# A new order of a kernel's pieces: score groups together, zeros up to the first transposes, later blocks of k loaded from SyncE's queue

## The chip, the core and the metric

The kernel runs on one core of a Trainium2 chip. The metric is device time in microseconds (us); the program launches once per run. The core has a matrix engine (TensorE, PE in the profile, with PEld for its weight loads), a vector engine (VectorE, DVE), an activation engine (ScalarE, ACT), a general engine (GpSimd, POOL) and SyncE (SP), which here only issues DMAs. Each works through its own list of instructions in order, and they wait for each other by semaphores. Matmul results go to PSUM, eight banks of 512 floats in each of 128 partitions.

## The reference

Two layers follow each other: a recurrent attention with decay, and a channel mix.

```python
for t in range(S):                       # q, k, v: 4 batches, 8 heads, 768 tokens, 64 wide
    state = gamma * state + outer(k[t], v[t])
    y[t] = 0.125 * q[t] @ state
x = y, heads side by side                # 4 x 768 x 512
x_prev = x shifted by one token
xk = mu_k * x + (1 - mu_k) * x_prev      # xr the same with mu_r
k = relu(xk @ w_k)                       # 512 -> 1024
out = sigmoid(xr @ w_r) * ((k * k) @ w_v)
```

## The kernel before

The 4 x 768 tokens are cut into 12 blocks n of 256 tokens, three to a batch. The recurrence is done in chunks of 128 tokens (u = 0 and 1 of a block): scores within a chunk, masked, and a state carried from chunk to chunk.

All work is cut into pieces, and the constant `ORDER` (lines 16 to 68) is the list of them, written out by hand: a loop at its end (lines 518 to 530) calls one function for each word. Every engine executes its pieces in the order of the words, and nothing reorders them. A word is a code, its numbers, and after @ the PSUM banks that it writes; T.4.1@0 is the transposition of k of block 4 into bank 0. The codes are:

- lk, lq, lv (lines 178 to 185): load k, q, v of a block. k stays in 32 bits; q and v are cast to 16 bits on the way. lk.n alone is issued by SP, lk.n.2 by POOL, lq and lv always by POOL. There are four buffers of each. wk, wr, wv, mu: weights and mixing factors (wk and wv in two halves), from POOL; mu from ACT.
- ks: k scaled by powers of the decay, on VectorE for blocks 0 to 2, on POOL from 3 on. gy: a table of powers, on VectorE.
- T.n.1 and Tq.n: PE transposes k (128x128) and q (64x64); E.n.1 and E.n.0 copy these to SBUF on ACT.
- S.n.i: scores of block n (i: even or odd tokens as keys), I.n: the part of y from the carried state; C.n: the new state; Y.n: the rest of y. All are runs of 64x64 matmuls on PE.
- M.n.i: VectorE masks the scores. U.n.u and G.n.u: state summed (VectorE) and decayed (POOL). D.n: y scaled into x. dx.n: x minus its neighbour (POOL, VectorE for blocks 0 and 1). X.n.w.j0.j1: VectorE mixes xk (w = 0) or xr (w = 1), columns j0 to j1.
- K.n.g: keys, eight matmuls of 128x256; Q.n.g: relu and square on ACT. R.n.t: gate; s.n.t: its sigmoid on ACT. V.n.t.p: values, first or second half of the sum. O.n.t: product on VectorE; st.n.t: store, from SP.
- Block 0 has the halves apart (Du, du, Xu, Ku, Qu), block 11 its last product (Vc, Oc, sc). S.0 and T.0 are in two halves.
- z.c: c matmuls of zeros whose result nobody reads (lines 481 to 486). mt, me: mu transposed by PE and copied by ACT.

In SBUF, ks, qT, kT, the masked scores, xk and xr have three buffers each, dx two, the gates and outputs five. A piece that writes a PSUM bank waits until what was in it has been read. DMAs from POOL use eight semaphores in turn, so each waits until the one eight before it has landed.

Of the kernel before, what the change touches and what calls it, by code (L numbers as in the profile page):

```python
# [13 lines left out]

KSC = 64.0
ORDER = """
lk.0.0.0.2 lk.0.0.2.4 lq.0 mu lv.0 gy wk.0 lk.1.2 ks.0.0.0.2 z.7@0 mt@0 lq.1 me ks.0.0.2.4
T.0.1.0.2@1 lv.1 E.0.1.0.2 T.0.1.2.4@0 E.0.1.2.4 wk.1 z.2@2 Tq.0@23 wr E.0.0 wv.0 z.4@4
S.0.0.0.2@23 C.0@01 wv.1 M.0.0.0.2 S.0.0.2.4@45 M.0.0.2.4 U.0.0 z.5@6 I.0.0@45 U.0.1 S.0.1.0.2@23
S.0.1.2.4@67 lk.2.2 M.0.1.0.2 M.0.1.2.4 G.0.1 z.5@0 Y.0 ks.1.0 lq.2 Du.0.0 z.4@1 T.1.1@6 lv.2  # L20
Tq.1@23 du.0.0.0 E.1.1 Xu.0.1.0.0.1 z.2@0 C.1@01 lk.3.2 Xu.0.1.0.3.4 E.1.0 Xu.0.1.0.2.3
Xu.0.1.0.1.2 Xu.0.0.0.3.4 Xu.0.0.0.0.1 z.2@7 S.1.0@23 Xu.0.0.0.1.2 M.1.0 lq.3 Xu.0.0.0.2.3 U.1.0
z.7@4 Ku.0.0.0@4 Du.0.1 G.1.0 du.0.0.1 I.1.0@23 Qu.0.0.0 S.1.1@67 Ku.0.1.0@0 Xu.0.1.1.0.1
Xu.0.1.1.2.3 lv.3 Xu.0.1.1.1.2 R.0.0@4 Xu.0.1.1.3.4 Qu.0.1.0 Xu.0.0.1.3.4 Xu.0.0.1.0.1
Xu.0.0.1.1.2 R.0.1@0 Xu.0.0.1.2.3 s.0.0 M.1.1 Ku.0.1.1@5 s.0.1 lk.4.2 U.1.1 Y.1 Qu.0.1.1 G.1.1
Ku.0.0.1@1 D.1 V.0.0.0@0 Qu.0.0.1 lq.4 dx.1.0 V.0.0.1 V.0.1.0@1 X.1.1.3.4 lv.4 X.1.1.1.2 X.1.1.2.3
V.0.1.1 X.1.1.0.1 ks.2.0 R.1.0@2 lq.5 Tq.2@45 X.1.0.0.1 s.1.0 T.2.1@3 X.1.0.1.2 lk.5.2 E.2.0 C.2@2
X.1.0.2.3 R.1.1@6 U.2.0 E.2.1 X.1.0.3.4 O.0.0 G.2.0 K.1.3@7 s.1.1 O.0.1 ks.3.1 st.0.0 I.2.0@23
Q.1.3 S.2.1@45 st.0.1 S.2.0@01 M.2.1 K.1.0@6 lv.5 T.3.1@7 M.2.0 Q.1.0 C.3@45 lq.6 K.1.1@6 E.3.1
U.3.0 lk.6.2 U.3.1 Y.2 Q.1.1 ks.4.1 Tq.3@67 D.2 K.1.2@5 E.3.0 V.1.0.0@4 Q.1.2 dx.2.1 S.3.0@67  # L30
I.3.0@23 S.3.1@01 M.3.0 T.4.1@5 V.1.0.1 G.3.1 E.4.1 M.3.1 lk.8.2 V.1.1.0@6 X.2.1.2.3 lv.6 V.1.1.1
X.2.1.3.4 X.2.1.1.2 lk.7.2 C.4@01 X.2.1.0.1 Y.3 X.2.0.1.2 lq.7 R.2.0@5 X.2.0.2.3 X.2.0.3.4
X.2.0.0.1 lv.7 R.2.1@7 s.2.0 U.4.0 O.1.1 G.4.0 K.2.1@5 s.2.1 O.1.0 ks.5.1 st.1.1 Tq.4@67 D.3 Q.2.1
st.1.0 K.2.2@0 E.4.0 U.4.1 K.2.0@5 dx.3.1 Q.2.2 I.4.0@67 S.4.1@01 S.4.0@23 Q.2.0 M.4.1 T.5.1@4
ks.6.1 K.2.3@5 E.5.1 M.4.0 V.2.0.0@0 Q.2.3 G.4.1 V.2.1.0@1 lk.9.2 X.3.1.0.1 X.3.1.1.2 V.2.0.1
X.3.1.3.4 lq.8 X.3.1.2.3 V.2.1.1 X.3.0.0.1 lk.10.2 X.3.0.3.4 Y.4 X.3.0.2.3 X.3.0.1.2 C.5@5 Tq.5@23
U.5.0 ks.8.1 K.3.3@4 E.5.0 O.2.1 O.2.0 K.3.0@5 st.2.1 Q.3.3 D.4 st.2.0 G.5.0 K.3.1@4 Q.3.0 ks.7.1
I.5.0@01 S.5.0@67 S.5.1@23 Q.3.1 M.5.0 T.6.1@5 K.3.2@4 E.6.1 dx.4.1 M.5.1 V.3.0.0@6 Q.3.2 R.3.1@7
lk.11.2 X.4.1.1.2 V.3.1.0@4 X.4.1.0.1 s.3.1 X.4.1.2.3 lv.8 R.3.0@7 X.4.1.3.4 X.4.0.0.1 lq.9
X.4.0.2.3 R.4.1@5 s.3.0 X.4.0.1.2 X.4.0.3.4 V.3.1.1 s.4.1 K.4.1@5 O.3.1 K.4.3@7 st.3.1 Q.4.1  # L40
C.6@45 Tq.6@23 Q.4.3 U.6.0 ks.9.1 Y.5 U.6.1 V.3.0.1 E.6.0 D.5 K.4.2@7 G.6.1 O.3.0 dx.5.1 S.6.0@01
Q.4.2 st.3.0 I.6.0@23 S.6.1@45 M.6.0 R.4.0@6 T.7.1@7 M.6.1 s.4.0 lv.9 K.4.0@0 E.7.1 lq.10
X.5.1.2.3 T.8.1@1 X.5.1.3.4 Q.4.0 Y.6 X.5.1.1.2 C.7@67 X.5.1.0.1 lv.10 Tq.7@45 E.8.1 X.5.0.1.2
V.4.0.0@0 X.5.0.0.1 lq.11 E.7.0 X.5.0.2.3 V.4.0.1 X.5.0.3.4 U.7.0 ks.10.1 D.6 K.5.2@1 K.5.3@6
Q.5.2 O.4.0 G.7.0 K.5.1@1 st.4.0 Q.5.3 dx.6.1 U.7.1 V.4.1.0@0 Q.5.1 K.5.0@6 G.7.1 R.5.1@1 Q.5.0
X.6.1.0.1 X.6.1.1.2 S.7.0@67 X.6.1.2.3 I.7.0@23 s.5.1 S.7.1@45 X.6.1.3.4 V.4.1.1 M.7.0 R.6.0@1
X.6.0.2.3 V.5.1.0@6 X.6.0.0.1 s.6.0 X.6.0.3.4 V.5.1.1 X.6.0.1.2 O.4.1 V.5.0.0@7 O.5.1 st.4.1 M.7.1
V.5.0.1 st.5.1 R.5.0@6 Y.7 s.5.0 Tq.8@45 O.5.0 lv.11 C.8@6 K.6.1@0 E.8.0 U.8.0 st.5.0 D.7 G.8.0
K.6.3@1 Q.6.1 ks.11.1 I.8.0@45 S.8.1@23 Q.6.3 S.8.0@67 M.8.1 K.6.0@0 dx.7.1 K.6.2@1 M.8.0 Q.6.0
# [12 lines left out]
Q.10.3 Y.11 K.10.2@3 D.11 R.9.1@0 Q.10.2 dx.11.1 R.10.1@3 s.9.1 K.10.1@4 s.10.1 X.11.1.0.1
V.9.0.0@3 Q.10.1 X.11.1.3.4 X.11.1.1.2 K.9.2@4 X.11.1.2.3 X.11.0.2.3 V.10.0.0@5 X.11.0.1.2 Q.9.2
X.11.0.0.1 V.10.1.0@4 X.11.0.3.4 K.11.3@0 V.10.0.1 Q.11.3 V.10.1.1 O.10.0 K.11.1@0 st.10.0 O.10.1
R.11.0@1 st.10.1 Q.11.1 K.11.0@0 s.11.0 V.9.0.1 Q.11.0 V.9.1.1 O.9.0 K.11.2@0 st.9.0 O.9.1
R.11.1@1 st.9.1 Q.11.2 V.11.0.0@0 s.11.1 V.11.0.1 Vc.11.1.0@1 O.11.0 Vc.11.1.1@2 st.11.0 Oc.11.1.0
sc.11.1.0.0 Oc.11.1.1 sc.11.1.1.1
"""


# [1 line left out]
def kernel(  # L72
# [13 lines left out]
    B, H, S, D = q.shape  # L86
# [3 lines left out]
    C = 128  # L90
    TM = 2 * C
    NJ = H // 2
# [57 lines left out]
    ident = c16[:, 0:P]  # L150
# [45 lines left out]
    def turned(n, a, j0=0):  # L196
        return banks("T", n, a, j0).bitcast(F16)
# [14 lines left out]
                            Q16(n)[:, 2 * j + hp, i * D : i * D + D], ident,  # L212
                        )

    def trans_q(n):
        pt = turned(n, 0)[:, :, 0 : 2 * NJ * D].rearrange("p u (j i t) -> p u j i t", j=NJ, i=2)
        for j in range(NJ):
            for i in range(2):
                for u in range(2):
                    r = slice(u * D, u * D + D)  # L220
                    for hp in range(2):
                        nc.tensor.transpose(  # L222
                            pt[hp * D : hp * D + D, u, j, i, :],
                            Q16(n)[r, 2 * j + hp, i * D : i * D + D], ident[r, r],
                        )

    def transed(n, a, j0=0, j1=NJ):
        pt = turned(n, a, j0)
        if len(BANK["T", n, a, j0]) == 2:
            pt = pt[:, :, 0 : 2 * NJ * D].rearrange("c u (j i p) -> c u j p i", j=NJ, i=2)  # L230
            out = QT(n).rearrange("c j u (p i) -> c u j p i", i=2)
        elif a == 0:
            pt = pt.rearrange("c (j i p) -> c j p i", j=NJ, i=2)[:, j0:j1]
            out = QT(n)[:, j0:j1].rearrange("c j u (p i) -> c j (u p) i", i=2)
        else:
            pt = pt.rearrange("c (j i p) -> c j i p", j=NJ, i=2)[:, j0:j1]
            out = KT(n)[:, j0:j1]
        nc.scalar.copy(out=out, in_=pt)  # L238
# [265 lines left out]
    def load_wv(h):  # L504
# [5 lines left out]
        "S": scores, "M": masked, "C": state, "U": summed, "G": decayed, "I": inter, "Y": intra,  # L510
        "D": yout, "dx": differ, "X": mixed, "K": keys, "Q": squared, "R": gate, "s": opened,
        "V": values, "O": result, "st": store, "gy": powers, "wk": load_wk, "wr": load_wr,
        "wv": load_wv, "mu": load_mu, "mt": trans_mu, "me": copy_mu, "z": zeros, "Tq": trans_q,
        "Du": yout_u, "du": differ_u, "Xu": mixed_u, "Ku": keys_u, "Qu": squared_u,
        "Vc": values_c, "Oc": result_c, "sc": store_c,
    }
# [1 line left out]
    for word in ORDER.split():  # L518
        word, _, at = word.partition("@")
        code, *args = word.split(".")  # L520
        args = tuple(int(x) for x in args)
        if at:
            key = args
            if code in ("T", "Tq"):
                code_key, key = "T", (args[0], args[1] if code == "T" else 0, (args[2:] + (0,))[0])
            else:
                code_key = code
                key = {"I": args[:1], "S": args[:2] + (args[2:] + (0,))[:1]}.get(code, args)
            BANK[(code_key,) + key] = [int(x) for x in at]
        CODES[code](*args)  # L530
# [30 lines left out]
```

## Time and profile before

| | us |
|---|---|
| median of 3 runs | 162.99 (162.97, 162.99, 164.17) |
| the profiled execution | 164.16 |
| its span | 162.4 |
| PE busy in it | 153.6 |
| VectorE busy | 116.5 |
| ACT busy | 94.3 |
| POOL busy | 80.5 |

The profile is of one execution. A start time counts from the beginning of the span. In a group's line stand its start, the time from the first start to the last end, engine, line, operation, tiles and count; in square brackets is how long the engine had been idle and what released it. Matmuls overlap, so a group's length is more than its distance to the next group. In the lines by slices each digit is the busy share of one fortieth of the span in tenths.

### The profile page before, as it was taken

What the parts mean: (1) busy time and instruction counts of PE and PEld (TensorE: products, weight loads), DVE (VectorE), ACT (ScalarE), POOL (GpSimd) and SP (SyncE); (2) the same over time, 40 slices, a digit from 0 to 9 for tenths busy, and PEclk for the clock granted to TensorE, in tenths of its full rate; (3) what the DMA queues carried; (4) which work ended last, traced back from release to release, by engine and by line L of the source; (5) the groups of instructions that cost most, each with busy time, mean ns of one, the idle gap of its engine ahead of it and who ended that gap; (6) DMA issues with size and microseconds to landing.
All of it is one profiled execution on the core that took longest, in us unless ns stands there. A gap on an engine that the chain in (4) does not pass through costs nothing.

```text
span 162.4 us, 5592 instructions
## 1 busy us (share of the span) xinstructions
PE 153.6 (95%) x2479; PEld 99.4 (61%) x2479; DVE 116.5 (72%) x209; ACT 94.3 (58%) x148; POOL 80.5 (50%) x79
## 2 busy tenths in 40 slices
PE   7499999999999999999969999999999999999992
PEld 2245577458657668566836558458568668666661
DVE  2518997988598688948997957927998979364222
ACT  3230438378727929767829418686467937774740
POOL 7938435629999969909786009303216140130000
PEclk9999999999999999999999999999999999999999
DMA  5999999999999989294694036211030011000333
GB/s 149 168 254 197 205 211 249 247 246 253 269 230 229 239 167 299 39 215 129 81 172 96 4 129 111 23 69 65 6 124 10 4 69 40 25 4 0 129 129 129
DMA packets 34167, 21.98 MB, mean 135 GB/s; under 512 B 25816, under 2 KB 29792, under 8 KB 34144
## 3 DMA queue, kind: packets, MB, share of 16 engines
q0 software_dynamic: 29184, 14.68, 60.7%
q1 hardware_dynamic: 4512, 6.69, 11.5%
q8 instruction: 19, 0.31, 0.8%
q10 hardware_dynamic: 448, 0.26, 0.6%
q14 instruction: 4, 0.03, 0.1%
HBM read 24.25 MB, written 6.29 MB: 188 GB/s over the span
## 4 chain that ended last, share of the span: by engine, by line
PE 81%; DVE 7%; ACT 5%; DMA 2%; issue 1%; ACTq 1%; POOL 0%; DVEq 0%
PE ps L395 23%; PE ps L421 22%; PE ps L409 12%; PE ps L246 5%; PE ps L483 4%; PE ps L315 3%; PE ps L204 3%; PE ps L302 3%; DMA mu<-in_moe_mu_r_dram 2%; DVE xk L358 2%; PE ps L222 2%; ACT qT L238 2%; PE ps L271 2%; ACT kr L402 1%; PE ps L375 1%
## 5 line engine op out<-in xcount | busy, mean ns | idle before, releaser
L395 PE MATMUL ps<-xk,wk 128*128 128x256 f16 x352 | 44.1, 273 | 1.7 <-DVE xk L358 1.6
L421 PE MATMUL ps<-wv,k 128*128 128x512 f16 x184 | 43.7, 379 | 0.0
L395 PEld LDWEIGHTS <-wk 128*128 128x128 f16 x352 | 33.4, 98 | 10.2 <-issue 2.1
L253 DVE TENSOR_TENSOR a<-ps,c_sb 128x1024 f16<-128x1024 f32 (+1 forms) x26 | 28.8, 1138 | 13.3 <-PE ps L246 6.5
L402 ACT ACTIVATE kr<-ps 128x512 f32<-128x512 f32 x44 | 26.1, 593 | 18.0 <-PE ps L395 18.0
L344 POOL TENSOR_TENSOR dx<-xT 128x1024 f32<-128x1024 f32 x10 | 18.9, 1892 | 20.3 <-DVE xT L329 20.3
L405 ACT ACTIVATE k<-kr 128x512 f16<-128x512 f32 x44 | 27.7, 630 | 1.4
L421 PEld LDWEIGHTS <-k 128*128 128x128 f16 x184 | 17.3, 98 | 18.3 <-ACT k L405 0.4
L427 DVE SCALAR_TENSOR_TENSOR os<-ps,rs 128x512 f32<-128x512 f32 x23 | 15.4, 686 | 14.5 <-PE ps L421 5.9
L415 ACT ACTIVATE rs<-ps 128x512 f32<-128x512 f32 x24 | 14.2, 593 | 18.4 <-PE ps L409 15.2
L409 PE MATMUL ps<-wr,xr 128*128 128x512 f16 x96 | 23.9, 380 | 0.0
L358 DVE SCALAR_TENSOR_TENSOR xr<-dx,mu,xT 128x256 f16<-128x256 f32 (+1 forms) x52 | 21.0, 465 | 4.0 <-POOL dx L344 3.9
L358 DVE SCALAR_TENSOR_TENSOR xk<-dx,mu,xT 128x256 f16<-128x256 f32 (+1 forms) x52 | 23.4, 510 | 0.0
L189 POOL TENSOR_TENSOR ks<-k,csm_sb 128x1024 f16<-128x1024 f32 x9 | 17.1, 1905 | 5.1 <-PE ps L271 5.1
L290 POOL TENSOR_TENSOR tg<-t,csm_sb 128x256 f16<-128x256 f32 x16 | 10.0, 622 | 18.2 <-DVE t L287 18.1
L238 ACT COPY kT<-ps 128x1024 f16<-128x1024 f16 (+1 forms) x13 | 12.1, 940 | 8.7 <-PE ps L204 8.7
L176 POOL DMA_DIRECT2D v<-in_v_dram x12 | 10.9, 906 | 11.5 <-PE ps L222 9.1
L329 DVE TENSOR_TENSOR xT<-ps,gy_sb 128x1024 f32<-128x1024 f32 x11 | 13.4, 1219 | 4.1 <-ACT kr L402 2.9
L238 ACT COPY qT<-ps 128x1024 f16<-128x1024 f16 x12 | 12.1, 1007 | 6.1 <-PE ps L222 6.1
L409 PEld LDWEIGHTS <-xr 128*128 128x128 f16 x96 | 8.8, 98 | 9.1 <-DVE xr L358 0.3
L483 PE MATMUL ps<-zero 128*128 128x512 f16 x38 | 13.0, 480 | 1.2 <-DVE xT L467 1.2
L176 POOL DMA_DIRECT2D q<-in_q_dram x12 | 11.0, 913 | 2.5 <-DMA wk<-in_moe_w_k_dram 1.6
(43 smaller groups left out, 142.4 us busy)
## 6 DMA issues: line engine op xcount, KB each, us to landing
out_dram<-os SPq DMA_DIRECT2D x23, 256.0 KB, 2.1
k<-in_k_dram POOLq DMA_DIRECT2D x11, 512.0 KB, 8.6
q<-in_q_dram POOLq DMA_DIRECT2D x12, 256.0 KB, 8.1
v<-in_v_dram POOLq DMA_DIRECT2D x12, 256.0 KB, 7.3
wk<-in_moe_w_k_dram POOLq DMA_DIRECT2D x2, 512.0 KB, 10.8
wv<-in_moe_w_v_dram POOLq DMA_DIRECT2D x2, 512.0 KB, 16.6
k<-in_k_dram SPq DMA_DIRECT2D x2, 256.0 KB, 3.5
wr<-in_moe_w_r_dram POOLq DMA_DIRECT2D x1, 512.0 KB, 14.4
```

The costliest lines, as they stand in the source:

```text
L176: eng.dma_start(out=d(n)[:, 2 * j0 : 2 * j1], in_=rows(x, n)[:, 2 * j0 : 2 * j1])
L189: (nc.vector, nc.gpsimd)[e].tensor_tensor(out=KS(n)[:, :, h0:h1], in0=K32(n)[:, h0:h1].rearrange("p h (i d) -> p i h d", i=2), in1=gks[:, ...
L238: nc.scalar.copy(out=out, in_=pt)
L253: nc.vector.tensor_tensor(out=A2(n)[:, i, :, j0:j1], in0=pairs(banks("S", n, i, j0))[:, :, j0:j1], in1=causal[:, i, None, None, :].to_broa ...
L344: (nc.vector, nc.gpsimd)[e].tensor_tensor(out=DX(n)[:, j0:j1, t0:t1], in0=x[:, j0:j1, c + t0 : c + t1], in1=x[:, j0:j1, c - 1 + t0 : c - 1 ...
L358: nc.vector.scalar_tensor_tensor(out=XM[w](n)[:, j, t0:t1], in0=DX(n)[:, j, t0:t1], scalar=mu[:, w * NCO + j : w * NCO + j + 1], in1=x[:, ...
L395: nc.tensor.matmul(pz[:, i, :], lhsT=wk16[:, co, fo * P : fo * P + P], rhs=XM[0](n)[:, co, :], start=(i == 0 and co == 0), stop=(co == NCO ...
L402: nc.scalar.activation(out=kr, in_=banks("K", n, g).rearrange("p (i t) -> p i t", i=2), func=AF.Relu)
L405: nc.scalar.activation(out=K2(n)[:, 2 * g : 2 * g + 2], in_=kr, func=AF.Square)
L409: nc.tensor.matmul(banks("R", n, tb), lhsT=XM[1](n)[:, co, tb * P : tb * P + P], rhs=wr16[:, co, :], start=(co == 0), stop=(co == NCO - 1),)
L421: nc.tensor.matmul(banks("V", n, tb, 0), lhsT=K2(n)[:, fo, tb * P : tb * P + P], rhs=wv16[:, fo, :], start=(fo == 0), stop=(fo == NFO - 1),)
L483: nc.tensor.matmul(banks("z", count), lhsT=zero[:, 0:P], rhs=zero, start=True, stop=True, skip_group_check=True,)
```

## The change

The list `ORDER` is written anew; with the six pieces named below apart, every piece other than the zeros occurs in both lists with the same numbers, while banks and places differ. At the start:

```diff
-lk.0.0.0.2 lk.0.0.2.4 lq.0 mu lv.0 gy wk.0 lk.1.2 ks.0.0.0.2 z.7@0 mt@0 lq.1 me ks.0.0.2.4
-T.0.1.0.2@1 lv.1 E.0.1.0.2 T.0.1.2.4@0 E.0.1.2.4 wk.1 z.2@2 Tq.0@23 wr E.0.0 wv.0 z.4@4
-S.0.0.0.2@23 C.0@01 wv.1 M.0.0.0.2 S.0.0.2.4@45 M.0.0.2.4 U.0.0 z.5@6 I.0.0@45 U.0.1 S.0.1.0.2@23
-S.0.1.2.4@67 lk.2.2 M.0.1.0.2 M.0.1.2.4 G.0.1 z.5@0 Y.0 ks.1.0 lq.2 Du.0.0 z.4@1 T.1.1@6 lv.2
+lk.0.0.2.4 lk.0.0.0.2 lq.0 lv.0 lv.1 lk.1.2 ks.0.0.2.4 lq.1 ks.0.0.0.2 wk.1 gy z.10@1 T.0.1.0.2@0
+T.0.1.2.4@1 E.0.1.0.2 wk.0 mu wr z.4@4 Tq.0@23 E.0.1.2.4 lk.2.2 E.0.0 wv.0 z.5@4 S.0.0.0.2@23
+S.0.0.2.4@01 C.0@45 M.0.0.0.2 U.0.0 lq.2 M.0.0.2.4 z.2@6 I.0.0@23 S.0.1.0.2@67 U.0.1 S.0.1.2.4@01
+M.0.1.0.2 G.0.1 M.0.1.2.4 ks.1.0 z.5@4 Y.0 Du.0.0 z.1@4 C.1@01 mt@6 U.1.0 T.1.1@2 Du.0.1 G.1.0 me
```

The two halves of S.0.0 follow each other, and C.0 comes after both. S.1.0, I.1.0 and S.1.1 follow each other, where a group of keys stood between the first two. Y, C and Tq of a block and its neighbours stand together in most blocks. mt and its load move behind the first transposes. On PE the order around blocks 0 to 4 becomes:

```diff
-z.7@4 Ku.0.0.0@4 I.1.0@23 S.1.1@67 Ku.0.1.0@0 R.0.0@4 R.0.1@0 Ku.0.1.1@5 Y.1 Ku.0.0.1@1 V.0.0.0@0
-V.0.0.1 V.0.1.0@1 V.0.1.1 R.1.0@2 Tq.2@45 T.2.1@3 C.2@2 R.1.1@6 K.1.3@7 I.2.0@23 S.2.1@45 S.2.0@01
-K.1.0@6 T.3.1@7 C.3@45 K.1.1@6 Y.2 Tq.3@67 K.1.2@5 V.1.0.0@4 S.3.0@67 I.3.0@23 S.3.1@01 T.4.1@5
+I.1.0@45 S.1.1@67 Ku.0.1.1@0 Ku.0.0.1@2 z.1@3 Ku.0.0.0@0 R.0.0@2 Y.1 T.2.1@3 Ku.0.1.0@0 V.0.1.0@0
+V.0.0.0@1 R.0.1@4 Tq.2@67 C.2@3 K.1.2@2 K.1.3@4 K.1.1@5 S.2.0@23 I.2.0@67 K.1.0@4 V.0.0.1 S.2.1@23
+T.3.1@4 V.0.1.1 Y.2 C.3@23 Tq.3@45 R.1.0@0 V.1.0.0@1 S.3.0@23 I.3.0@45 S.3.1@67 R.1.1@0 V.1.0.1
```

Later in the list, attention runs further ahead of the channel mix: 22 groups of keys, gates and values follow Y.11 in the list before, 32 in the new one. The loads of k of blocks 6 to 11 lose their .2, so SP issues them, among the stores:

```diff
-st.0.0 st.0.1 st.1.1 st.1.0 st.2.1 st.2.0 st.3.1 st.3.0 st.4.0 st.4.1
+lk.6 st.0.0 st.0.1 st.1.0 lk.7 st.1.1 lk.10 lk.8 lk.9 st.2.0 st.2.1 st.3.0 st.4.0 st.3.1 lk.11 st.4.1
```

POOL's list around blocks 2 to 4 becomes:

```diff
-lq.4 lv.4 lq.5 lk.5.2 G.2.0 ks.3.1 lv.5 lq.6 lk.6.2 ks.4.1 dx.2.1 G.3.1 lk.8.2 lv.6 lk.7.2 lq.7 lv.7 G.4.0 ks.5.1
+lv.4 lq.4 lq.6 G.2.0 ks.3.1 lk.5.2 lv.5 ks.6.1 G.3.1 ks.4.1 dx.2.1 lq.5 lv.7 lv.6 G.4.0 ks.5.1
```

The functions change only so that a code Tk, which transposes k in 64x64 pieces, would be understood. No word of the new list uses it.

```diff
-    def trans_q(n):
-        pt = turned(n, 0)[:, :, 0 : 2 * NJ * D].rearrange("p u (j i t) -> p u j i t", j=NJ, i=2)
+    def trans_small(n, a):
+        pt = turned(n, a)[:, :, 0 : 2 * NJ * D].rearrange("p u (j i t) -> p u j i t", j=NJ, i=2)
...
+    def trans_q(n):
+        trans_small(n, 0)
+
+    def trans_k(n):
+        trans_small(n, 1)
```

## The prediction

> **What bounds the kernel now.** I read the page's shares first, then the chain of waits, then TensorE's timeline and, beside it, what each DMA's issue says of its landing.
>
> ```profile
> span 162.4 us, 5592 instructions
> ...
> PE 153.6 (95%) x2479; PEld 99.4 (61%) x2479; DVE 116.5 (72%) x209; ACT 94.3 (58%) x148; POOL 80.5 (50%) x79
> ...
> PE   7499999999999999999969999999999999999992
> ...
> DVE  2518997988598688948997957927998979364222
> ...
> DMA  5999999999999989294694036211030011000333
> ...
> PE 81%; DVE 7%; ACT 5%; DMA 2%; issue 1%; ACTq 1%; POOL 0%; DVEq 0%
> ```
>
> TensorE holds the chain. From 22 us on it hardly idles: eight key matmuls take 0.87 us per group, four value or gate matmuls 0.86, wherever they stand. Such work can't shrink by reordering; only holes, filler and switches can. The filler stands in the first 22 us (timeline of PE):
>
> ```profile
> 1.19 3.17 PE L483 MATMUL ps<-zero 128*128 128x512 f16 x7 [1.19 <-DVE xT L467]
> 6.46 0.24 PE L476 MATMUL ps<-csm_sb,mu 8*128 8x8 f32 x1 [2.10 <-DMA mu<-in_moe_mu_r_dram]
> 6.63 1.03 PE L204 MATMUL ps<-c_sb,ks 128*128 128x128 f16 x8
> 7.46 1.06 PE L483 MATMUL ps<-zero 128*128 128x512 f16 x2
> 8.45 0.64 PE L222 MATMUL ps<-c_sb,q 64*64 64x64 f16 x32
> 9.02 1.89 PE L483 MATMUL ps<-zero 128*128 128x512 f16 x4
> 10.84 0.43 PE L246 MATMUL ps<-qT,kT 64*64 64x128 f16 x8
> 11.84 1.69 PE L483 MATMUL ps<-zero 128*128 128x512 f16 x5
> 14.02 1.25 PE L483 MATMUL ps<-zero 128*128 128x512 f16 x5
> ```
>
> Seven zeros end, TensorE idles 2.10 us for mu, and the zeros stay slow: successive starts are 427 ns apart until 12.67 us and 217 ns after 12.94. The first scores (I call their start s, 10.84 here) come 0.69 us after their last input, the copy of qT that ends at 10.15; four slow zeros stand in between.
>
> One stall is no property of the order:
>
> ```profile
> 80.03 4.33 DVE L358 SCALAR_TENSOR_TENSOR xk<-dx,mu,xT 128x256 f16<-128x256 f32 x4
> 84.41 2.45 PE L395 MATMUL ps<-xk,wk 128*128 128x256 f16 x21 [1.62 <-DVE xk L358]
> ```
>
> One of these four took 3.15 us instead of 0.48, and TensorE's group 2.65 instead of 0.87: 1.78 us. The profiled execution was 164.16 (span 162.4 plus 1.76 around it); without that stall 162.4, against the median 162.99. I count changes from 162.99, since two of the three times are 162.97 and 162.99; from 162.4 all would be 0.6 lower.
>
> **The change, part by part.**
>
> Start up to s. `mt` and its wait leave the front; ten zeros of 0.427 us run from 1.19 to 5.46. The scaling of k now precedes `gy`: the loads land at 3.96 and 5.07 (issue 0.74 and 1.21, 3.2 and 3.9 to landing), so the two 0.69 us scalings end near 4.7 and 5.8, and T starts at 5.86 instead of 6.63. On ACT mu's two issues (0.58 + 0.27) now stand between the two copies of kT: the second ends near 8.3 to 8.6. Tq waits for q, which lands at 7.52 (1.25 + 6.26). Copying qT takes 1.0, so s can't be before 9.3 to 9.55. Whether it gets there depends on the zeros between Tq and the scores, five now: 2.1 us slow, 1.1 fast.
>
> [...] The row: 6.2 us of work from 6.46 came before the fast pitch. If that repeats from 5.86, z.4 and z.5 are slow, Tq ends at 9.0 and s is 11.1, 0.3 later than now. [...] I take release by 8 us at 3 in 4: s moves by -1.3 (ends -1.5 and +0.3).
>
> From s to block 4. Worked on each queue from the rows (M half 0.60, ks 1.13, half D 0.70, Xu 0.264, X 0.397, full D or M 1.14, E 0.9, Q 1.17, ks on POOL 1.87): U.0.0 ahead of the second M ends at s+1.6 rather than s+2.2; ks.1.0 ends at s+5.1, not s+5.6; D.1 starts at s+15.65 with ks.2.0 done already, where now it starts at s+16.85 without. VectorE is thus nearly 2 us ahead. TensorE is not: it waits 0.6 us for xk before Ku.0.1.1, 0.5 for bank 2, 0.4 for xk before Ku.0.0.0, and 0.85 at V.0.1.0@0, which follows Ku.0.1.0@0 in the same bank and has the 0.6 us relu with two handovers in front of it. T.4.1 starts at s+33.9 with V.1.0.1 done; now at s+33.2 without it (0.86). Net gain 0.16.
>
> POOL's early pieces, in the order of landing. Saturated, its queue spaces landings by 1.55 us for a k, 1.24 for a q, 1.5 for a v and 2.55 for a weight. v1 now goes ahead of k1, and wk's halves behind q1, so k1 lands near 12.7 (needed for ks.1.0 at s+3.9, 13.4), q1 13.9 (Tq.1, 15.8), wk.1 16.5 (Ku.0.1.1, 19.7), wk.0 19.1 (21.1), wr 21.7 (R.0.0, 23.3), k2 23.2 (ks.2.0, 23.7), wv.0 25.8 (V.0.1.0, 27.3). Least cover is 0.5 us, at k2; a late k2 would hold VectorE's U.1.1 and D.1, and through dx.1.0 the keys of block 1. An issue also waits for the landing of the issue eight before it: G.0.1 now stands behind q2, which waits for v1 (about 11.1) and is issued by 12, before U.0.1 is done (s+2.6). G.1.0 stands in front of v2, k3 and wv.1 and waits for U.1.0 (s+6.1, 15.7); those transfers would start moving only after wv.0 anyway, so it costs nothing. ks.6.1 ahead of G.3.1 and ks.4.1 waits for C.3 on TensorE and for lk.6; behind it are G.3.1, ks.4.1 and dx.2.1, and for ks.4.1 waits T.4.1: counted among the rivals.
>
> VectorE's late pieces. X.11.0 comes right behind D.11 and waits some 2 us for POOL's dx.11.1 (1.89), with three pieces of X.10.0 behind it. K.10.0 needs these 5.3 us after Y.11; seven groups (6.0 us) stand before it. Nothing lost, 0.7 of cover.
>
> Switches. A group ahead of a run of 64x64 matmuls takes 0.96 instead of 0.86, so a switch costs 0.1 us. The runs go from 33 to 30: 0.3 us, most of it inside the 0.16 above. Zeros go from 38 to 37, which by itself is nothing, as they fill waits.
>
> Block 4 to the end. Now the small holes are 0.41 at I.4.0 with 0.1 to 0.2 beside it. In the new order I find C.6@23 0.17 (Q.3.2 ahead of Q.3.3 on ACT), V.4.0.0 0.27, I.7.0@23 0.2, V.5.1.0@6 0.3, K.7.2 0.15, R.9.0@1 0.16, V.10.0.0 0.15: 1.4, against 0.6, less what the first blocks save at I.4.0. At S.8.0 the new order stands, work for work, 0.25 ahead of the old relative to s, and loses about 0.3 by the end: zero. The tail is the same work behind Vc; its wait for Q.11.3 is covered by R.11.0 and V.11.0.0 (1.73 against 1.3).
>
> k from SP. Six issues of 0.91 leave POOL: 5.4 us, all where POOL has slack (it waits 20.3 us for xT and 18.1 for t in all), so worth nothing directly. [...] Cover 0.2 and 0.9; ends 0 and +1; I take 0. Behind lk.6 on SP stand only stores, the first due at 38 us; lk.8 to lk.10 hold store 2.0 no longer than ks.5.1 (s+42, store due at s+49).
>
> Sum: -1.3 + 0.0 = -1.3: 161.7.
>
> **The rivals.**
>
> Clock released late. For it: the row above. Against: the 2.1 us idle is gone. s = 10.8 to 11.1: 162.9 to 163.3, no change.
>
> Just-in-time handovers lost, on the slower side. The new order leaves many arrivals with under 0.1 us: ks.4.1 behind ks.6.1 and G.3.1 on POOL (4.3 us of work in the 4.7 between C.3 and T.4.1), K.2.1 on xk, S.6.0 on U.6.1, R.4.1 on U.7.0, K.7.0 on its relu, about a dozen. Each late one stalls TensorE and all behind it, since nothing is reordered. From 0.11 us each the gain is gone; between 0.16 and 0.41, the two like waits of now (Tq.3 on ACT's kr at 41.0 us; I.4.0), it costs 1.9 to 4.9: 163.6 to 166.6, and as not all slip I put 164.9. For it: DVE shares of 8 and 9 until 125 us. Against: the present order is as tight and lost 1 us.
>
> [...]
>
> The change does less than it says: the small-transposition of k is coded but no word of the order uses it, and three switches fewer is 0.3 us. If also the zeros change nothing, 163.
>
> More gain: s = 9.3 from the 162.4 base, or a stall like that at 81 us seldom: 160.8.
>
> **How the numbers follow.** Clock early and handovers held 0.50 (161.7, own range 160.9 to 162.5); clock late or little changed 0.20 (163.0); handovers or loads lost 0.20 (164.9); more gain 0.10 (160.8). A measurement of this kernel tells about 1% (1.6 us) from no change. Faster by over 1% is under 161.36: a third of the first case, most of the last, and a little for the uncertain base: 0.30. Slower is over 164.62: most of the third and a rest: 0.19. Range 160.5 to 164.7.
>
> **What the changed profile would show.** Zeros at a 217 ns pitch before 9 us, T at 5.9, first scores at 9.3 to 9.6; Ku.0.1.0 and V.0.1.0 with a hole of 0.8 between; T.4.1 near 43.5; a store or k of SP landing in 6 us or more before 45 us; POOL with some 75 us busy. Wrong if scores start after 10.8, if holes of over 0.2 us on PE sum to more than 2 us after 45 us, or if TensorE waits for wv or v.

## The result, and the profile after

The changed kernel takes 161.34 us (median; 160.77 to 161.76) against 162.98 for the kernel before on the same chip: 0.9884 of it, 95% interval 0.9843 to 0.9925. A second series gave 161.33 against 163.09, 0.9894 (0.9859 to 0.993). So it gains 1.6 to 1.8 us, close to the 1% that counts as told apart from no change. The forecast was 161.7.

The profiled execution of after took 161.76, that of before 164.16. The latter lay 1.2 us above its own median, so distances between these two traces are too large by about that much, and I read places rather than totals from them. Both traces of the changed kernel are the slowest executions of their series (161.76 of four, 162.03 of six), so waits read from them are those of a late execution. From the page of after:

```profile
span 159.5 us, 5601 instructions
...
PE 151.9 (95%) x2478; PEld 98.8 (62%) x2478; DVE 116.7 (73%) x209; ACT 93.6 (59%) x148; POOL 75.1 (47%) x73
...
DMA  5999999999999999475159991100030000510153
...
PE 65%; DMA 18%; DVE 7%; POOL 5%; issue 2%; POOLq 0%; DVEq 0%
```

The last line is the one to stop at. DMA's share of the chain has gone from 2% to 18%. GpSimd is busy 75.1 us, as forecast. The chain in order of time (start, length, what) names two transfers:

```profile
6.53 12.81 DMA wk<-in_moe_w_k_dram
...
22.17 16.05 DMA q<-in_q_dram
...
38.27 0.44 PE ps L221 x32
```

The second is q of block 3: GpSimd issued it at 22.17, it landed at 38.22, and Tq.3 starts on it 0.05 later. Here is TensorE's timeline, the start first and then the places where it stood still before block 4, with the group in which a wait was forecast:

```profile
1.19 4.45 PE L494 MATMUL ps<-zero 128*128 128x512 f16 x10 [1.19 <-DVE xT L478]
5.89 1.03 PE L203 MATMUL ps<-c_sb,ks 128*128 128x128 f16 x8 [0.25 <-DVE ks L188]
6.71 1.10 PE L494 MATMUL ps<-zero 128*128 128x512 f16 x4
7.97 0.45 PE L221 MATMUL ps<-c_sb,q 64*64 64x64 f16 x32 [0.16 <-DMA q<-in_q_dram]
8.35 1.25 PE L494 MATMUL ps<-zero 128*128 128x512 f16 x5
9.54 0.42 PE L257 MATMUL ps<-qT,kT 64*64 64x128 f16 x16
...
24.68 0.62 PE L203 MATMUL ps<-c_sb,ks 128*128 128x128 f16 x8 [0.29 <-DVE ks L188]
25.13 1.06 PE L386 MATMUL ps<-xk,wk 128*128 128x128 f16 x16
26.03 1.89 PE L432 MATMUL ps<-wv,k 128*128 128x512 f16 x8
...
38.27 0.44 PE L221 MATMUL ps<-c_sb,q 64*64 64x64 f16 x32 [0.67 <-DMA q<-in_q_dram]
```

The start went as forecast: transposes at 5.89, zeros at the fast pitch of 217 ns from 7.0 us on, first scores (s) at 9.54 against 10.84. (The page's clock row reads 9 in every slice, before and after, so it is the pitch that shows the change.) But two holes follow that the forecast's sum did not have: 0.29 at T.2.1, for which it had only named k of block 2 as its least cover, and 0.67 at Tq.3. And one that it had is not there: V.0.1.0 at 26.03 follows Ku.0.1.0 at 25.13 without a wait. That is a misreading of mine. The list has Ku.0.1.0@1; the prediction, and the diff shown ahead of it, have @0.

Events by trace, in us (landings are the issue's start plus the trace's time to landing):

| | s | k of block 2 landed | T.2.1 | q of block 3 landed | Tq.3 | T.4.1 | end of PE |
|---|---|---|---|---|---|---|---|
| before | 10.84 | 28.34 | 33.29 | 33.79 | 41.03 | 44.03 | 159.17 |
| after | 9.54 | 23.37 | 24.68 | 38.22 | 38.27 | 43.00 | 156.15 |
| after, second series | 10.04 | 24.41 | 25.72 | 38.53 | 38.57 | 43.30 | 156.47 |

T.4.1 in after stands with V.1.0.1 (0.86 us of TensorE) already done, in before without it.

### The profile page after: what moved, and what is told of

Its sections match the earlier page's. It is cut to its first block, busy times and chain, and to the rows that moved or that the text cites. A ratio compares the mean times of both kernels' runs of the same rounds, so it can differ in the third digit from the quotient of the medians.

```text
span 159.5 us, 5601 instructions
## 1 busy us (share of the span) xinstructions
PE 151.9 (95%) x2478; PEld 98.8 (62%) x2478; DVE 116.7 (73%) x209; ACT 93.6 (59%) x148; POOL 75.1 (47%) x73
## 4 chain that ended last, share of the span: by engine, by line
PE 65%; DMA 18%; DVE 7%; POOL 5%; issue 2%; POOLq 0%; DVEq 0%
PE ps L432 21%; PE ps L406 19%; PE ps L420 11%; DMA q<-in_q_dram 10%; DMA wk<-in_moe_w_k_dram 8%; DVE xr L369 4%; PE ps L257 3%; PE ps L326 3%; PE ps L203 2%; PE ps L313 2%; POOL v L175 2%; PE ps L221 2%; PE ps L282 1%; DVE xk L369 1%; POOL q L175 1%
## 5 line engine op out<-in xcount | busy, mean ns | idle before, releaser
L432 PE MATMUL ps<-wv,k 128*128 128x512 f16 x184 | 45.2, 379 | 0.1
L406 PE MATMUL ps<-xk,wk 128*128 128x256 f16 x352 | 42.6, 273 | 0.1
L406 PEld LDWEIGHTS <-wk 128*128 128x128 f16 x352 | 33.9, 98 | 7.3
L369 DVE SCALAR_TENSOR_TENSOR xr<-dx,mu,xT 128x256 f16<-128x256 f32 (+1 forms) x52 | 25.3, 518 | 2.1 <-POOL dx L355 2.1
L420 PE MATMUL ps<-wr,xr 128*128 128x512 f16 x96 | 24.8, 379 | 0.5 <-DVE xr L369 0.5
L369 DVE SCALAR_TENSOR_TENSOR xk<-dx,mu,xT 128x256 f16<-128x256 f32 (+1 forms) x52 | 22.9, 478 | 3.0 <-POOL dx L355 3.0
L494 PE MATMUL ps<-zero 128*128 128x512 f16 x37 | 11.5, 451 | 1.2 <-DVE xT L478 1.2
## 6 DMA issues: line engine op xcount, KB each, us to landing
k<-in_k_dram SPq DMA_DIRECT2D x6, 512.0 KB, 11.3
```

The source lines that it names most:

```text
L369: nc.vector.scalar_tensor_tensor(out=XM[w](n)[:, j, t0:t1], in0=DX(n)[:, j, t0:t1], scalar=mu[:, w * NCO + j : w * NCO + j + 1], in1=x[:, ...
L406: nc.tensor.matmul(pz[:, i, :], lhsT=wk16[:, co, fo * P : fo * P + P], rhs=XM[0](n)[:, co, :], start=(i == 0 and co == 0), stop=(co == NCO ...
L420: nc.tensor.matmul(banks("R", n, tb), lhsT=XM[1](n)[:, co, tb * P : tb * P + P], rhs=wr16[:, co, :], start=(co == 0), stop=(co == NCO - 1),)
L432: nc.tensor.matmul(banks("V", n, tb, 0), lhsT=K2(n)[:, fo, tb * P : tb * P + P], rhs=wv16[:, fo, :], start=(fo == 0), stop=(fo == NFO - 1),)
```

## The experiments

My theory on going in was that of the forecast: the earlier s is the gain, all that follows moves with it, and k issued from SyncE is worth nothing. The rivals: the front is held by deliveries, whatever s is; and k from SyncE is itself the gain.

**The start alone, in the old order.**

```diff
-lk.0.0.0.2 lk.0.0.2.4 lq.0 mu lv.0 gy wk.0 lk.1.2 ks.0.0.0.2 z.7@0 mt@0 lq.1 me ks.0.0.2.4
+lk.0.0.2.4 lk.0.0.0.2 lq.0 lv.0 wk.0 lk.1.2 ks.0.0.2.4 ks.0.0.0.2 gy z.10@4 lq.1
...
+mt@7 me T.1.1@6
```

> The order of before with nothing but the changed start: k loaded and scaled ahead of gy, ten zeros straight up to the transposes, mu and its transposition behind them. Theory (the start sets when the first scores begin, and all that follows comes earlier by as much): first scores at 9.5 to 9.8 us instead of 10.84, time 161.6 to 161.8 against 163.0 for before (ratio near 0.992). Rival (the gain comes from the order behind the start): scores early, but the time stays at 162.6 to 163.2, since weights or k arrive no earlier and the wait only moves.

162.41 (162.06 to 163.17), 0.9964 of before (0.9935 to 0.9993): 0.6 to 0.8 gained, not 1.3. s came at 8.78, T.4.1 at 41.30, 2.7 earlier than in before's trace, so in the old order the front does follow the start: q of block 3 landed at 33.80 there, long before Tq.3 asked for it at 38.3. Then a part was lost in the middle of one group of keys, and the profile names nothing that the engine waited for (TensorE's timeline of this kernel):

```profile
49.13 1.04 PE L394 MATMUL ps<-xk,wk 128*128 128x256 f16 x8
51.45 0.50 PE L394 MATMUL ps<-xk,wk 128*128 128x256 f16 x3 [1.28 <-issue]
```

What made that wait is open, and so is whether other executions have it; this one, 162.38, is at the median.

**The old start in the changed order**: seven zeros, the wait for mu in front again, and two and four zeros behind the transposes.

```diff
-lk.0.0.2.4 lk.0.0.0.2 lq.0 lv.0 lv.1 lk.1.2 ks.0.0.2.4 lq.1 ks.0.0.0.2 wk.1 gy z.10@1 T.0.1.0.2@0
+lk.0.0.0.2 lk.0.0.2.4 lq.0 mu lv.0 gy lv.1 lk.1.2 ks.0.0.0.2 z.7@6 mt@6 me lq.1 ks.0.0.2.4 wk.1
```

> The changed order with the start of before: mu and gy first, seven zeros, the wait for mu in front of the transposes. Theory (start worth 1.3, the rest worth 0.3 to 0.6): first scores at 10.6 to 11.0, time 162.4 to 162.7 (ratio 0.996 to 0.998). Rival (the rest carries the gain): 161.3 to 161.6.

161.46 (161.09 to 161.71), 0.9905 (0.9876 to 0.9935): the changed kernel's time. TensorE:

```profile
10.69 0.42 PE L257 MATMUL ps<-qT,kT 64*64 64x128 f16 x16
...
25.48 0.62 PE L203 MATMUL ps<-c_sb,ks 128*128 128x128 f16 x8
...
38.15 0.49 PE L221 MATMUL ps<-c_sb,q 64*64 64x64 f16 x32
```

s is 1.15 later than in after, T.2.1 0.80 later, and Tq.3 0.12 earlier. The brackets are empty: with the late start there is no hole at T.2.1 or Tq.3. T.4.1 is at 42.93 against 43.00. From s to T.4.1 it takes 32.24 us here, 33.46 and 33.26 in the two traces of the changed kernel. So the start's lead was spent on waiting for k of block 2 and q of block 3. The forecast's "s moves by -1.3, and all follows" falls here. Executions with an earlier first landing keep a part of the lead: two kernels below (the order as I had misread it, and score groups pulled apart) have the changed start, the same loads and the first q at 7.65 and 7.12, where after has 7.93 and this kernel 7.46; their T.4.1 is at 42.32 and 42.06. At the medians, 161.46 and 161.34, nothing can be told.

**Three zeros instead of ten.**

```diff
-z.10@1 T.0.1.0.2@0
+z.3@1 T.0.1.0.2@0
```

> The changed order with three zeros instead of ten before the first transposes, nothing else. TensorE then idles from 2.5 to 5.9 us, but no piece has to wait longer for its inputs. Clock theory (the zeros release the fast pitch by 8 us): zeros still 427 ns apart until about 12 us, first scores at 10.7 to 11.1, time 162.5 to 162.9. Rival (the start gains by what was moved out of the transposes' way, and the zeros do nothing): first scores at 9.5 to 9.8, time 161.2 to 161.5.

```profile
1.19 1.46 PE L494 MATMUL ps<-zero 128*128 128x512 f16 x3 [1.19 <-DVE xT L478]
5.87 1.03 PE L203 MATMUL ps<-c_sb,ks 128*128 128x128 f16 x8 [3.21 <-DVE ks L188]
6.69 1.91 PE L494 MATMUL ps<-zero 128*128 128x512 f16 x4
...
9.11 1.92 PE L494 MATMUL ps<-zero 128*128 128x512 f16 x5
10.95 0.42 PE L257 MATMUL ps<-qT,kT 64*64 64x128 f16 x16
```

The transposes start at nearly the same time, 5.87, but four zeros now take 1.91 instead of 1.10 and five 1.92 instead of 1.25; the pitch changes at 10.4 us, where two starts lie 280 ns apart, against 6.7 in after. s is 10.95, 1.4 later. The forecast's theory on the pitch holds in the main: zeros stay slow to 10.4 us where it had about 12. The time is 161.87 (161.34 to 163.11), 0.9936 (0.99 to 0.9971), by medians and ratios 0.5 to 0.8 above the changed kernel's, where I had expected 162.5 to 162.9. In the traces T.4.1 is at 43.19 against 43.00 and nothing more is lost behind it; where the slower ones of the ten executions lost time is not shown.

**k of blocks 6 to 11 from GpSimd again**, in the same places of the list.

```diff
-lk.6
+lk.6.2
```

and so for 7 to 11.

> The changed order with k of blocks 6 to 11 issued by POOL again, at the same places in the list. Theory (the loads from SP add nothing, POOL has the 5.4 us to spare): 161.1 to 161.7, and q of block 3 lands no later than 38.2 us. Rival (moving the six loads to SP is part of the gain): 162.0 or more, with POOL's decays or its scaling of k late for TensorE.

162.39 (162.25 to 162.79), 0.9965 (0.9942 to 0.9988) against 0.9884 and 0.9894: 1.0 to 1.3 us of the gain come from this part alone. The trace, whose PE ends 1.07 later than that of after, shows the price in two places. The first is T.4.1:

```profile
43.32 0.62 PE L203 MATMUL ps<-c_sb,ks 128*128 128x128 f16 x8 [0.24 <-POOL ks L188]
```

From GpSimd's queue k of block 6 lands at 38.77 instead of 35.96; ks.6.1 waits for it, ks.4.1 stands behind ks.6.1 and ends at 43.27, and T.4.1 is 0.32 later than in after. The other is further on. GpSimd, then TensorE:

```profile
51.83 1.84 POOL L175 DMA_DIRECT2D k<-in_k_dram  x2
53.66 1.93 POOL L355 TENSOR_TENSOR dx<-xT 128x1024 f32<-128x1024 f32 x1
```

```profile
61.00 0.41 PE L257 MATMUL ps<-qT,kT 64*64 64x128 f16 x15 [0.43 <-DVE xT L340]
```

Two issues of 0.92 us stand ahead of dx.3.1, VectorE waits 0.9 us for dx and is late with all behind it, and TensorE stands 0.43 at S.5.0; by then it is 1.07 late, and it loses no more. "All where POOL has slack" was an average; in this stretch it has none. At the same time q of block 3 landed at 35.43, not 38.22, with the same issue time (22.18): in after, the SyncE load of k of block 6 had pushed GpSimd's queue back, by 2.79 us at this transfer.

**k of block 6 later.**

```diff
-U.1.1 lk.6 T.2.1@3
+U.1.1 T.2.1@3
...
-st.0.1 ks.6.1 R.1.0@0
+st.0.1 lk.6 R.1.0@0
...
-G.4.0 R.2.0@7
+G.4.0 ks.6.1 R.2.0@7
```

> The changed order, with only the load of k of block 6 moved from 24.65 us to behind the stores of block 0 on SyncE, and the GpSimd step that reads it (ks.6.1) moved behind G.4.0. Theory (the start's gain is lost at Tq.3, where q of block 3 lands at 38.22 because the SyncE load shares the DMA engines with GpSimd's queue): q of block 3 lands near 35.4, as it did with k of 6 on from GpSimd, the 0.67 us hole at Tq.3 is gone, T.4.1 stands near 42.4 instead of 43.0, and the median is 160.6 to 160.8. Rival (a wait of equal size comes next, at T.4.1 or T.5.1): T.4.1 or first K.3 at the same 43.0 and 58.1, median 161.3.

161.19 (160.85 to 162.12), 0.9888 (0.9857 to 0.9919): no gain that can be told. q of block 3 landed at 36.20, and the hole at Tq.3 went, as expected. But the profiled execution is the slowest of nine; its first q landed at 8.12, k of block 2 at 24.19, and the hole at T.2.1 was 0.92, so T.4.1 came at 43.01. Further on, ks.6.1 (1.9 us) in its new place did to dx.3.1 what the two issues had done: GpSimd

```profile
49.16 3.76 POOL L188 TENSOR_TENSOR ks<-k,csm_sb 128x1024 f16<-128x1024 f32 x2
52.88 0.60 POOL L301 TENSOR_TENSOR tg<-t,csm_sb 128x256 f16<-128x256 f32 x1
53.45 1.89 POOL L355 TENSOR_TENSOR dx<-xT 128x1024 f32<-128x1024 f32 x1
```

where dx starts at 50.94 in after. S.5.0 waited 0.43 here too, and from T.4.1 to PE's end it takes 113.95 instead of 113.15. The rival (a wait of equal size comes next) was right, at another place than it named.

**The same with T.2.1 behind Ku.0.1.0.**

```diff
-U.1.1 T.2.1@3 D.1 G.1.1 Ku.0.1.0@1 lv.4
+U.1.1 D.1 G.1.1 Ku.0.1.0@1 T.2.1@3 lv.4
```

> The kernel with k of block 6 later, and besides T.2.1 moved from behind U.1.1 to behind Ku.0.1.0, so that the GpSimd step it waits for (ks.2.0) has 0.9 us more. Theory: its 0.29 us hole is gone too and nothing later takes it up, since q of block 3 has landed by then: about 0.3 under the kernel with k of block 6 later alone, 160.3 to 160.5. Rival (the next landing or GpSimd's next product takes it up): the same time as that kernel.

161.67 (161.06 to 162.04), 0.9895 (0.9868 to 0.9923): the same. VectorE, then TensorE:

```profile
23.65 1.22 DVE L188 TENSOR_TENSOR ks<-k,csm_sb 128x1024 f16<-128x1024 f32 x1 [0.99 <-DMA k<-in_k_dram]
```

```profile
25.26 1.05 PE L386 MATMUL ps<-xk,wk 128*128 128x128 f16 x16 [1.26 <-DVE t L298]
```

ks.2.0 is on VectorE (I had taken it for GpSimd's), and VectorE waits there for the load with U.1.1 and D.1 behind it. U.1.1 reads bank 1, which Ku.0.1.0@1 writes. Moving the reader on TensorE only moved the wait to the next group.

**The order as I had misread it.**

```diff
-Ku.0.1.0@1 lv.4 Xu.0.1.1.3.4 V.0.1.0@0 dx.1.0 Qu.0.1.0 V.0.0.0@1
+Ku.0.1.0@0 lv.4 Xu.0.1.1.3.4 Qu.0.1.0 V.0.1.0@0 dx.1.0 V.0.0.0@1
```

> The changed order as I had misread it: Ku.0.1.0 in bank 0, its reader Qu.0.1.0 ahead of V.0.1.0, which takes the same bank. Theory: a hole of 0.7 to 0.9 us before V.0.1.0 at 26 us, as priced, but taken up at Tq.3, which waits until 38.2 for q of block 3 anyhow (its hole goes from 0.67 to nothing): T.4.1 at 43.0 to 43.2, median 161.3 to 161.6. Rival (holes add, as my sum has them): T.4.1 near 43.85, median 162.1 to 162.2.

```profile
26.39 0.38 PE L432 MATMUL ps<-wv,k 128*128 128x512 f16 x1 [0.69 <-ACT kr L394]
...
37.54 0.44 PE L221 MATMUL ps<-c_sb,q 64*64 64x64 f16 x29
```

The hole exists in that order, 0.69 us against the 0.85 that I had priced, and the time doesn't show it: 161.26 (161.06 to 161.31), 0.9875 (0.9827 to 0.9924). In this execution it was covered in part. q of block 3 landed at 37.07, and Tq.3 started 0.47 later; in the kernel that follows next, without the hole, q landed at 37.06 and Tq.3 started at 37.10. So some 0.3 of the hole was taken up by the wait for q and 0.4 was not. A hole before a fixed arrival is free as far as the arrival is later.

**Score groups pulled apart** in blocks 3 to 11.

```diff
-S.4.0@67 lk.8 I.4.0@45 Q.2.2 dx.3.1 S.4.1@01 lk.9 V.2.1.0@2 M.4.1
+S.4.0@67 lk.8 Q.2.2 dx.3.1 lk.9 V.2.1.0@2 I.4.0@45 S.4.1@01 M.4.1
```

> The changed order with the group of 64-row pieces of each of blocks 3 to 11 pulled apart: S.n.0 first, then the next full-row piece, then I.n and S.n.1, so two more passages between 64-row and 128-row pieces a block, some 18 in all (9 more groups). Theory (a switch costs about 0.1 us a group, as the prediction's sum has it): 0.9 us more, PE's end near 157.0, median 162.2. Rival (a switch costs nothing where weight loads run ahead): 161.3 to 161.4.

166.06 (165.0 to 166.38), 1.016 of before (1.01 to 1.0221): 4.7 us slower than after, where I expected 0.9. Its trace, of the fastest of four executions, ends 3.1 later on TensorE; from T.4.1 on it takes 117.22 us against 113.15. Of these 4.07, holes make 1.43 (2.03 against 0.60). TensorE's two longest waits there:

```profile
PE ps L419 <- DVE xr L368: 0.7, 1, 0.7
PE ps L419 <- DVE a L263: 0.4, 1, 0.4
```

The columns are who waited for whom, us in total, times, longest; a are the masked scores, which now come late. The passages themselves: measured in after as the distance of first matmuls beyond the usual pitch, a step into 64-row pieces costs 0.093 us (median of 17) and a step out of them 0.142, together 0.235 a group, not 0.1. Eight groups more behind 44 us are 1.9. Blocks 9, 10 and 11, where pulling apart makes no new hole, lose 0.22 to 0.23 each, as this says. The rest, 0.8, I can't assign.

**q of block 3 ahead of v of block 3**, on GpSimd's queue.

```diff
-S.1.0@23 lv.3 Xu.0.0.1.3.4
+S.1.0@23 lq.3 Xu.0.0.1.3.4
...
-Xu.0.1.0.3.4 lq.3
+Xu.0.1.0.3.4 lv.3
```

> The changed order with only the loads of v and of q of block 3 exchanged on GpSimd's queue. Theory (deliveries of GpSimd's queue, one after the other, set Tq.3): q of block 3 lands near 36.8 in the place of v, the hole at Tq.3 goes, U.3.0 does not wait for v at 38.2 since it stands 3 us behind Tq.3: T.4.1 near 42.3, median 0.5 to 0.7 under the changed kernel. Rival (something else, such as VectorE, holds the same place): T.4.1 at 43.0, the same time.

q landed at 35.57, v at 37.11, and the wait changed hands:

```profile
37.15 0.45 PE L280 MATMUL ps<-v,ks 64*64 64x64 f16 x32 [0.23 <-DMA v<-in_v_dram]
```

C.3, which reads v and stands just ahead of Tq.3, now waits 0.23; I had thought of U.3.0 as v's first reader. T.4.1 was at 42.17, 0.83 earlier than in after, PE's end at 155.35. That is not the exchange's doing: the first q landed at 7.30, and in the two kernels just shown, with v ahead and first landings of 7.65 and 7.12, the later of v and q came at 37.07 and 37.06, as here. The median, 161.28 (160.76 to 162.07; 0.9891, 0.9852 to 0.9929), is that of the changed kernel beside it,

> The changed kernel once more, as the level beside which the three others of this series stand. Every theory: 161.2 to 161.5.

which came to 161.33. The profiled execution is the fastest of six here (160.76), and the slowest of six of the changed kernel beside it (162.03); a few tenths gained in the front are below what these runs tell.

**ks.6.1 in GpSimd's idle time.** As k of block 6 later, with ks.6.1 moved on:

```diff
-G.4.0 ks.6.1 R.2.0@7
+G.4.0 R.2.0@7
...
-X.3.0.2.3 lq.7 V.2.0.1
+X.3.0.2.3 lq.7 ks.6.1 V.2.0.1
```

> As the kernel with k of block 6 later, but ks.6.1 (1.88 us on GpSimd) stands behind the load of q of block 7, where GpSimd was idle for 3.98 us from 54.6, and no longer between G.4.0 and dx.4.1. Theory (that kernel gained 0.67 at Tq.3 and gave 0.87 back at K.3.1 and S.5.0 because dx.3.1 came 1.9 to 2.5 us later on GpSimd and VectorE waited 1.0 for it): no hole at S.5.0, T.4.1 to PE's end 113.15 again instead of 113.95, T.4.1 near 42.3, median 0.6 to 0.8 under the changed kernel of the same series, 160.5 to 160.8. Rival (the SyncE load's place is not what made q of block 3 late; T.4.1 stays near 43): the same as the changed kernel.

In this place ks.6.1 stands behind the load of k of block 10, which takes the same buffer: it reads k of block 10 in the place of block 6's. The amount of work is the same, but its wait is another's. GpSimd, then TensorE:

```profile
57.95 1.90 POOL L186 TENSOR_TENSOR ks<-k,csm_sb 128x1024 f16<-128x1024 f32 x1 [4.14 <-DMA k<-in_k_dram]
```

```profile
60.47 0.30 PE L311 MATMUL ps<-qT,tg 64*64 64x128 f16 x4 [1.55 <-POOL tg L299]
```

What it does show is the front: q of block 3 at 35.15, no hole at T.2.1 (k of block 2 at 22.74) nor at Tq.3, s at 9.20, T.4.1 at 41.56, 1.44 earlier than in after. From s to T.4.1 it takes 32.36, against 32.24 with the old start, whose s was 1.49 later: with deliveries out of the way the start's lead does arrive at block 4. (k of block 2 is loaded as in the changed kernel; that it came earlier is the execution's luck.) S.5.0, at 58.50, is still 1.43 earlier than in after. Then 1.55 was lost to the late k, and the median is 161.1 (160.57 to 161.66; 0.9879, 0.9842 to 0.9916). With the load of k of block 10 behind ks.6.1 that hole should go; this was not run.

**k of block 2 ahead of wr as well**, with R.0.0 moved behind T.2.1 (and ks.6.1 as in the kernel just shown, reading k of block 10).

```diff
-E.0.1.0.2 wk.0 mu wr z.4@4 Tq.0@23 E.0.1.2.4 lk.2.2 E.0.0 wv.0
+E.0.1.0.2 wk.0 mu lk.2.2 wr z.4@4 Tq.0@23 E.0.1.2.4 E.0.0 wv.0
...
-M.1.1 R.0.0@2 Qu.0.0.0
+M.1.1 Qu.0.0.0
...
-D.1 G.1.1 Ku.0.1.0@1
+D.1 G.1.1 R.0.0@2 Ku.0.1.0@1
```

> As e9 (k of block 6 later, ks.6.1 in GpSimd's idle time), and k of block 2 ahead of wr on GpSimd's queue, with R.0.0, the first reader of wr, moved behind T.2.1. Theory (T.2.1 starts 1.31 us after k of block 2 lands, whatever the start): k of block 2 lands near 21 and T.2.1 no longer waits, it starts 0.9 us after 'as soon as its engine is free', near 23.5 to 23.8, T.4.1 near 41.8 to 42.0, median 0.2 to 0.4 under e9. Rival (the bytes that must be there by V.0.1.0, wv of half 0, or by Tq.2 set the next wait): T.4.1 as in e9.

k of block 2 landed at 20.15, and T.2.1 still waited:

```profile
24.07 0.62 PE L201 MATMUL ps<-c_sb,ks 128*128 128x128 f16 x8 [0.50 <-DVE ks L186]
```

Now VectorE's own work ahead of ks.2.0 sets it: ks.2.0 starts at 22.79 without a wait. T.4.1 is at 42.29, later than in the kernel just shown, and then the late k of block 10 holds both at the same place (I.5.0 at 60.26 and 60.47). The time is 160.94 (160.48 to 161.53), 0.9865 (0.9827 to 0.9904): the lowest median of all, but within the interval of the changed kernel, and this kernel does not compute the reference's result.

## Why the prediction was right, and where it was not

The number, 161.7 against 161.34, and the range held. The sum under it (-1.3 from the start, 0 from the rest) did not, so that the number came out near is in good part luck: a gain that was put at nothing came in the place of one that mostly went. None of the three signs of being wrong that I had named showed; the wait that came, for q of block 3, was not among them.

- **The start up to s: right.** T 5.86 / 5.89, release by 8 / 7.0, s 9.3 to 9.55 / 9.54 (forecast / measured). Three zeros gave 10.95, so the ten are the cause of most of it (the first q landed 0.26 later there). That ten zeros would bring the fast pitch by 8 us was my estimate, and no trace of before showed it. The runs show this: with 4.4 us of zeros without a break the pitch changed at 6.7 us in after and by 5.9 in the start alone (the eight transposes at 5.90 took 0.62 instead of 1.03, the two zeros at 6.36 0.59), with 1.5 us of them only at 10.4. With seven zeros and the wait for mu it changed at 12.7 in before, but with the old start among the four zeros from 9.28, which took 1.47 instead of 1.89. So what sets the moment is not shown.
- **"s moves by -1.3 ... and all follows": wrong.** It failed in the step from s to block 4, where I compared times relative to s and gave the landings only as covers. T.2.1 starts 1.30 to 1.31 us after k of block 2 lands in both traces of the changed kernel and in those with k from GpSimd and with k of block 6 later (24.68 after 23.37; 25.72 after 24.41; 24.70 after 23.40; 25.50 after 24.19). Tq.3 starts 0.04 to 0.05 after q of block 3 lands (38.27 after 38.22; 38.57 after 38.53). With the old start both holes are gone and block 4 begins at the same time. That T.4.1 came at 43.00, near the forecast 43.5, is luck too: the hole of 0.85 that is not there stood for the 0.96 of the two that are.
- **GpSimd's landings: right to 0.3 us** as far as I took them (k of block 1 12.7 / 12.53, wk's first half 16.5 / 16.73, k of block 2 23.2 / 23.37, wv's first half 25.8 / 25.66). I stopped at wv's second half, which landed at 33.72, and never asked for q of block 3, two landings behind.
- **lk.6, "I take 0": wrong.** No run shows that term. Its covers, 0.2 and 0.9, were those of v of block 2 at C.2 and of wv's second half at V.0.0.1, against a push of GpSimd's queue by 1.55 us, an estimate of mine from the landings of before. Neither place shows idle time in after (v landed at 28.65, C.2 started at 28.98; wv at 33.72, V.0.0.1 at 33.76). The push was larger, and what it met came behind these two. From k of block 3 to q of block 3 it is 7.98 us in after, 7.24 in the second series and 7.30 with three zeros, and 5.26 to 5.30 in the four kernels with it later (30.94 to 36.20; 30.38 to 35.65), 5.29 with k from GpSimd: 2.0 to 2.7 us. That is the 0.67 at Tq.3. The piece I feared for, ks.6.1, was safe: k landed at 35.96, 11.3 us after issue.
- **k from SyncE "worth nothing directly": wrong.** It is worth 1.0 to 1.3 us. The step summed GpSimd's waits over the whole kernel instead of asking about ks.6.1 at 38 us and dx.3.1 at 51 us.
- **0.85 at V.0.1.0: a misreading**, as said. In an order that has it, it measured 0.69, of which some 0.4 was not covered.
- **Switches, 0.1 each: too small.** 0.235 a group; three groups fewer are 0.7, not 0.3, before what hides them.
- **Block 4 to the end: holes of 1.4 forecast.** With their size in after, as excess over the usual pitch: 0.16 at S.7.0 behind V.4.0.0, 0.25 at I.7.0, 0.24 at V.5.1.0, 0.18 at R.9.0, and 0.64 at R.6.0 (0.47 of it idle), which was not in the list; at C.6, K.7.2 and V.10.0.0 I find none. The dozen tight handovers of the slower rival held: no hole at T.4.1, K.2.1, S.6.0, R.4.1 or K.7.0.
- **The VectorE stall "no property of the order": wrong.** It is, as the last section shows, and the place where it meets TensorE accounts for about 1.1 us between the traces (1.62 at K.5.2 before, 0.47 at R.6.0 after).

So the gain of 1.6 in the medians is made up otherwise than I had it: 1.0 to 1.3 from k leaving GpSimd's list, 0.6 from order and start together (0.9965 with k on GpSimd). How the 0.6 divides between the start, fewer switches, the VectorE stall's place and small holes can't be told from these runs. The start alone gave 0.6 to 0.8 in the old order and nothing that can be told in the new one; neither the old order with k from SyncE nor the new one with the old start and k from GpSimd was run.

## What to carry to other kernels

An earlier start is worth what the next delivery leaves of it: between the traces of after and of the old start, 1.15 us of lead at the first scores was nothing at block 4. So list for each engine the arrivals it will meet in order, the last of them too, and carry the lead through them as a maximum and not as a sum. Before calling an engine's relief free because it idles for tens of us in all (here that relief was worth 1.0 to 1.3 us), look at the one stretch where it produces what another engine waits for. And where a repair only moves a reader (the wait of 0.92 at T.2.1 became one of 1.26 at Ku.0.1.0), see which in-order engine holds the wait.

## What the runs showed of the hardware

**A mixing piece of VectorE ended 0.28 to 0.30 us after the ks of GpSimd beside it.** The long VectorE instruction sits at the same word in every trace of one order: X.5.0.3.4 at 3.13 to 3.15 us in before and with the start alone, X.6.1.3.4 at 3.35 to 3.36 in all of the changed order. Before, VectorE and then GpSimd:

```profile
81.22 3.15 DVE L358 SCALAR_TENSOR_TENSOR xk<-dx,mu,xT 128x256 f16<-128x256 f32 x1
```

```profile
81.24 0.89 POOL L176 DMA_DIRECT2D q<-in_q_dram  x1
82.13 1.93 POOL L189 TENSOR_TENSOR ks<-k,csm_sb 128x1024 f16<-128x1024 f32 x1
```

And after, with the TensorE group that waits for it:

```profile
89.17 3.35 DVE L369 SCALAR_TENSOR_TENSOR xr<-dx,mu,xT 128x256 f16<-128x256 f32 x1
```

```profile
88.84 0.89 POOL L175 DMA_DIRECT2D q<-in_q_dram  x1
89.75 0.63 POOL L301 TENSOR_TENSOR tg<-t,csm_sb 128x256 f16<-128x256 f32 x1
90.32 1.91 POOL L188 TENSOR_TENSOR ks<-k,csm_sb 128x1024 f16<-128x1024 f32 x1
```

```profile
92.58 0.39 PE L420 MATMUL ps<-wr,xr 128*128 128x512 f16 x1 [0.47 <-DVE xr L369]
```

ks ends at 84.07 and VectorE's instruction at 84.36; ks at 92.23, VectorE's at 92.52. In each of the fourteen traces every mixing piece of VectorE that lies beside a ks of GpSimd ends 0.28 to 0.30 us after it, X.8.0.1.2 of the changed order with its 1.59 us too. Pieces of VectorE that read PSUM (masks, copies of x, products) lie beside the same GpSimd instructions with their usual 0.42, 0.68 and 1.22. The mixing pieces read dx and xT from SBUF. Why their ends go together is not shown, and the beginnings do not fit ks alone: the long piece of before starts 0.91 us before ks and by its usual 0.48 would have ended before ks began. GpSimd was issuing a load then, but three pieces beside the issue before it (v, at 80.38) kept their 0.48. So what held the piece until ks is open, and moving ks was not tried. That both orders meet this only once or twice shows how it can be looked for: beside each ks of GpSimd, which mixing piece of VectorE comes next?

**A 512 KB load from SyncE put GpSimd's queue back 2.0 to 2.7 us.** Beside that queue it took 10.0 to 11.3 us to land. In before, between 28 and 37 us, GpSimd's queue itself lands such a load 1.5 to 1.6 us after the transfer ahead of it (28.34 after 26.78, 32.55 after 31.09, 36.95 after 35.35), so the push was larger than the load's place in the queue would have been.

**The first landing carries through, in the main.** Between executions of the changed order the first q lands anywhere from 7.12 to 8.42 us, k of block 2 (in the kernels that load it in the same place) from 22.74 to 24.41, which is 15.2 to 16.2 us behind it. Differences of a few tenths in the front between single traces can be this, and no edit's doing.
